# Attention, soft routing and feed-forward in one kernel: another order of loads and steps, and the last weight block in column pieces

## Chip, cores and metric

The kernel runs on one core of one Trainium2 chip. The metric is the device time of the program in microseconds. TensorE (PE in the profile) does matmuls and transposes, VectorE (DVE), ScalarE (ACT) and GpSimd (POOL) work on elements, and SyncE (SP) issues the DMA transfers. PEld is PE's loading of the stationary operand.

## What is computed

Three layers follow one another. The first is windowed attention (4 batches, 8 heads, 576 positions, head size 64, window 64), the second a soft mixture of experts with 32 slots over 8 experts, the third a feed-forward layer with 2,048 hidden units. All 2,304 tokens of width 512 go through all three.

```python
scores = q @ k.T / 8;  keep only 0 <= pos_q - pos_k < 64
attn = exp(scores - max) / (sum + 1e-9);  x = attn @ v           # (2304, 512)

logits = x @ phi                                                 # (2304, 32)
d = softmax over the tokens;  slot_input = d.T @ x               # 8 experts x 4 slots x 512
h = maximum(slot_input[e] @ w1[e], 0);  slot_out[e] = h @ w2[e]  # w1 512x1024, w2 1024x512 for each e
c = softmax over the slots;  x = c @ slot_out                    # (2304, 512)

h = x @ w_in;  g = h * sigmoid(1.702 * h);  out = g @ w_out      # w_in 512x2048, w_out 2048x512
```

The softmax over the tokens needs all of attention, and the slots need that softmax. w_in and w_out come as 64-bit floats and are narrowed in the kernel.

## The kernel before

**Attention** runs in 18 steps (`work`): 16 units of one batch and one pair of heads with eight chunks of 64 rows each, and two steps for the ninth chunks. The steps are pipelined by hand: iteration i emits the scores of step i (`emit_s`, mask L315 and products L330 into bank "s"), the transposes of step i-1 (`emit_t`, PE L350, and its copies to `ab` by ACT L351, head 0 into tile `pa`, head 1 into `pl`), exp of head 0 (`emit_e`, ACT L342, with the running maximum `nm` of DVE L335), the transposes of the normalised rows of step i-2 (`xt_step`, PE L403, ACT L407), the values of step i-1 (`emit_pv`, PE L365), exp of head 1, and the normalisation of step i-1 (`emit_norm`, DVE L374 to L384). Pieces of the routing stand at steps by the tables `mid`, `early`, `late` and `post`: logits (PE L449) at 5, 9, 13 and 17, turns of the weights at 6, 10, 14, slots (PE L499) at 7, 11, 15.

**Order.** Every engine works off its instructions in the order in which the code emits them; nothing is scheduled by a planner. All loads are issued by SP, each behind what it waits for: Q and K of a pair (`load_qk`, L229, 512 KB; L231 for the ninth chunks), V (`load_v`, L243, 258 KB), raw blocks of w_in and w_out (`raw_load`, L154, 512 KB), and w1 and w2 (`load_w`, L149), 16 blocks of 1 MB each. A Q/K or V load waits until its buffer, one of three in turn, has been read. `W_AT` says how many weight blocks are issued at the end of each step; the rest go at fixed places of the tail and with each group of w1. A weight block takes one of 16 slots "w", of which three first hold raw blocks (`raws`), or for w2[0] to w2[6] a seventh of the `arena`, in which attention keeps Q, K, V, x and their transposes.

**Raw blocks** of w_in (four) and w_out (`N_WO`, two) are narrowed during attention: `CONV_AT` names the step at which ACT (L161) begins with each, then POOL, then three passes on DVE.

**The tail** (from `rings.update` behind the steps) ends the routing: values and normalisation of step 17, logits of the ninth chunks (`tail_logits`, PE L686), slots, their sum over the batches (`gather`, `acc`), the transposed slot inputs `siT`, and in between the transposes of the combine weights (`sides`; `c_tile`, PE L419, 32 matmuls for each batch). Then come four groups of w1 (`emit_w1`, PE L763), each behind four blocks, and 16 blocks of w2 (`emit_w2`, PE L804) that add up in one bank. The last w2 block is loaded in two halves of its columns. `so_turn` (PE L860) transposes the slot outputs into `soT`, and `emit_m2` and `emit_m1` (PE L893, L878) multiply them with w_in.

**The feed-forward part** runs 48 steps; each has a product L964, the gelu on ACT (L952), its second half on DVE (L977), and the products with w_out into the output banks (`emit_o`, PE L996). The w_out blocks that were not narrowed during attention are narrowed here (`out_a` on ACT L908, `out_b` on DVE L914 and L171 to L179, `out_w` on ACT L932, `out_c` on DVE L935).

## Time and profile before

| | before |
|---|---|
| runs, us | 370.49, 372.44, 372.84; median 372.44 |
| profiled execution, us | 372.59 |
| its span from the first to the last instruction, us | 370.6 |
| PE busy, us | 355.0 (96%) |
| DVE, ACT, POOL busy, us | 237.8, 195.6, 47.4 |
| mean granted TensorE clock | 1.00 |
| moved by DMA, MB | 70.87 |
| first product into the output (PE L996), us | 145.83 |

The profiled execution's own time is 2.0 us more than its span. Times in views count from the span's start. A busy PE in the first 140 us is the sum of many short matmuls and also of pieces that overlap; whether a wait there costs anything is read from the chain of waits and from the transfers.

### The profile page before, as it was taken

To read this page: it belongs to the slowest core of one execution; us is meant where nothing else is said; L and a number is where in the kernel's file an instruction comes from. 1 tells how busy PE (TensorE), PEld (TensorE's weight loads), DVE (VectorE), ACT (ScalarE), POOL (GpSimd) and SP (SyncE) were. 2 spreads that over 40 slices of the span, in tenths; PEclk is the share of its full clock that TensorE was granted. 3 is DMA by queue.
4 is the path that set the end of the run, shared out by engine and by line. 5 is a ranking of instruction groups with operands and counts; after the bars stand their busy time and mean duration, and the time that the engine had idled before them with its cause. 6 is when DMAs were issued, how large, how long until landed. Compare 5 with 4: busy or idle time off the path is not lost.

```text
span 370.6 us, 7867 instructions
## 1 busy us (share of the span) xinstructions
PE 355.0 (96%) x3091; PEld 271.5 (73%) x3091; DVE 237.8 (64%) x518; ACT 195.6 (53%) x498; POOL 47.4 (13%) x92
## 2 busy tenths in 40 slices
PE   6999999999789998999999999999999999999995
PEld 5887777768543325888778887788887888888884
DVE  3566788877356404949485969697968786262624
ACT  3798878879223205765666644555545453333330
POOL 4545666441100000000000000000000000000000
PEclk9999999999999999999999999999999999999999
DMA  7999999999999995314031314131300000031404
GB/s 268 334 404 408 412 413 409 406 381 375 398 385 370 424 392 218 107 57 135 38 113 58 113 57 130 42 113 59 113 0 2 0 0 2 0 136 37 165 6 170
DMA packets 18804, 70.87 MB, mean 191 GB/s; under 512 B 2000, under 2 KB 3408, under 8 KB 14800
## 3 DMA queue, kind: packets, MB, share of 16 engines
q1 hardware_dynamic: 18768, 70.38, 50.1%
q8 instruction: 24, 0.39, 0.4%
q14 instruction: 12, 0.10, 0.1%
HBM read 65.65 MB, written 4.72 MB: 190 GB/s over the span
## 4 chain that ended last, share of the span: by engine, by line
PE 75%; DMA 9%; ACT 8%; DVE 4%; issue 2%; SPq 0%; POOL 0%; DVEq 0%; ACTq 0%; POOLq 0%
PE s L996 18%; PE t L996 17%; PE v L996 17%; DMA w<-in_w_dram 8%; PE m L964 5%; PE v L365 3%; ACT pa L342 3%; PE s L330 3%; PE m L350 2%; DMA arena<-in_qk_dram 2%; ACT pl L351 2%; ACT pa L351 1%; PE m L499 1%; PE m L449 1%; PE s L763 1%
## 5 line engine op out<-in xcount | busy, mean ns | idle before, releaser
L952 ACT ACTIVATE r<-m 128x384 fp32r<-128x384 f32 (+1 forms) x97 | 47.5, 493 | 85.0 <-PE m L964 84.9
L977 DVE TENSOR_TENSOR r<-g,r 128x384 fp32r<-128x384 f32 x96 | 51.4, 554 | 51.3 <-ACT g L952 43.0
L996 PE MATMUL t<-w,r 128*128 128x512 f32 x288 | 75.8, 395 | 0.0
L996 PE MATMUL s<-w,r 128*128 128x512 f32 x288 | 74.3, 392 | 0.0
L996 PE MATMUL v<-w,r 128*128 128x512 f32 (+1 forms) x291 | 73.4, 387 | 0.0
L996 PEld LDWEIGHTS t<-w,r 128*128 128x128 f32 x288 | 53.8, 188 | 14.7 <-issue 4.0
L996 PEld LDWEIGHTS v<-w,r 128*128 128x128 f32 x291 | 54.3, 188 | 11.4
L996 PEld LDWEIGHTS s<-w,r 128*128 128x128 f32 x288 | 52.6, 188 | 8.5
L952 ACT ACTIVATE g<-m 128x384 f32<-128x384 f32 x96 | 47.9, 501 | 0.0
L342 ACT ACTIVATE pa<-s,nm 128x128 f32<-128x128 f32 x140 | 40.7, 399 | 6.2 <-DVE nm L335 5.7
L964 PE MATMUL m<-cT,w 128*128 128x384 f32 (+2 forms) x113 | 25.7, 319 | 0.0
L335 DVE TENSOR_REDUCE nm<-s 128x4 f32<-128x512 f32 x35 | 22.5, 684 | 4.3 <-PE s L330 3.0
L964 PEld LDWEIGHTS m<-cT,w 128*128 128x128 f32 x113 | 20.8, 188 | 4.7 <-DVE w L901 0.6
L350 PE MATMUL m<-ident,pa 128*128 128x128 f32 x144 | 19.6, 279 | 0.0
L351 ACT COPY pa<-m 128x512 f32<-128x512 f32 x18 | 10.5, 586 | 13.7 <-PE m L350 13.6
L350 PEld LDWEIGHTS m<-ident,pa 128*128 128x128 f32 x144 | 15.5, 141 | 3.0 <-issue 2.4
L330 PE MATMUL s<-arena 64*64 64x128 f32 x352 | 13.7, 271 | 2.2 <-POOL rawt L247 1.6
L763 PE MATMUL s<-w,phis 128*32 128x512 f32 x128 | 14.6, 595 | 0.5 <-DVE phis L744 0.5
L384 DVE TENSOR_TENSOR arena<-v,rs 128x256 f32<-128x256 f32 x36 | 13.6, 420 | 0.6
L330 PEld LDWEIGHTS s<-arena 64*64 64x64 f32 x352 | 11.4, 133 | 3.5 <-POOL rawt L247 2.0
L365 PE MATMUL v<-arena,pa 128*64 128x65 f32 x184 | 13.2, 227 | 0.3 <-issue 0.3
L1016 DVE TENSOR_TENSOR w<-s,w 128x512 f32<-128x512 f32 x18 | 11.6, 684 | 2.8 <-PE s L996 2.8
(206 smaller groups left out, 472.7 us busy)
## 6 DMA issues: line engine op xcount, KB each, us to landing
w<-in_w_dram SPq DMA_DIRECT2D x24, 1024.0 KB, 10.4
w<-in_w_out_dram SPq DMA_DIRECT2D x16, 512.0 KB, 3.4
arena<-in_w_dram SPq DMA_DIRECT2D x7, 1024.0 KB, 8.5
iraw<-in_w_in_dram SPq DMA_DIRECT2D x12, 512.0 KB, 3.3
arena<-in_qk_dram SPq DMA_DIRECT2D x10, 512.0 KB, 8.7
out_dram<-w SPq DMA_DIRECT2D x16, 256.0 KB, 2.1
arena<-in_vt_dram SPq DMA_DIRECT2D x13, 258.5 KB, 7.5
rawt<-in_qk_dram SPq DMA_DIRECT2D x6, 512.0 KB, 9.9
```

What stands on the lines that cost most here:

```text
L330: nc.tensor.matmul(st[h][rows[j], c, :], q, k, start=False, stop=(c == 3), tile_position=(64 * h, 64 * j))
L335: nc.vector.tensor_reduce(out=nm[:, h], in_=st[h], axis=AX.X, op=ALU.max, negate=True)
L342: nc.scalar.activation(out=pb[h][:, c, :], in_=st[h][:, c, :], func=ACTF.Exp, bias=nm[:, h, c:c + 1], scale=1.0)
L350: nc.tensor.transpose(tt[:, c, :], pb[h][:, c, :], ident)
L351: nc.scalar.copy(ab[h], tt)
L365: nc.tensor.matmul(pvt[i][h][64 * j:64 * j + 64, c, :], ab[h][:, c, 64 * j:64 * j + 64], v, start=True, stop=True, tile_position=(0, 64 * j))
L384: nc.vector.tensor_tensor(out=o, in0=pv[h][:, :, 1 - h:65 - h], in1=rs[:, h].unsqueeze(2).to_broadcast([128, 4, 64]), op=ALU.mult)
L763: nc.tensor.matmul(ph[32 * j:32 * j + 32, :], siT[:, kk, :], w1t[4 * r + j][:, kk, :], start=(kk == 0), stop=(kk == KD - 1), tile_position ...
L952: nc.scalar.activation(out=(gh, g)[part][:, a:e], in_=ph[:, a:e], func=ACTF.Gelu_apprx_sigmoid)
L964: nc.tensor.matmul(ph[:, c - a:e - a], mst[:, f * 128:f * 128 + 128], cT(c, e - c), start=True, stop=True)
L977: nc.vector.tensor_tensor(out=gl, in0=g, in1=gh.bitcast(F32), op=ALU.subtract)
L996: nc.tensor.matmul(accs[t][:, h], a[:, c], b[:, h], start=(first and k == 0), stop=(last and k == 2 and h.stop == 512))
```

## The change

- **Values.** `emit_pv` runs over the heads outside and the chunks inside.
- **Start.** The loads are issued in the order qk0, qk1, v0, qk2, v1. The scores of step 2 (with `scale_q(2)` on DVE in place of POOL) stand ahead of the values of step 0, and the three filler matmuls of that place are gone.
- **Raw blocks.** `N_WO` is 1. Two raw blocks are loaded ahead of the steps, two behind step 0 and one behind step 1. `CONV_AT` begins at steps 3, 5, 7, 9 and 11.
- **Weights by step.** `W_AT` gives none at step 10, two at 15, two at 16 and three at 17.
- **Arena.** X0, QK0, XT0, V0, X1, XLT0 and XL0 are each at the start of a seventh; the small tiles fill what is left, some move to `rawt`.
- **Tail.** The values of step 17 stand ahead of the transposes of the combine weights. For three batches `c_wide` spreads the weights with one DVE copy and four full transposes take the place of 32 narrow matmuls. Slots come behind the second tail logits; `acc` is scaled on ACT, and `siT` is copied in two halves by ACT and DVE.
- **Last w2 block.** It is laid out on the host by 128 columns and loaded in pieces of 256, 128 and 128 columns. Blocks 0 to 13 add up in one bank, which ACT copies; blocks 14 and 15 go by pieces into three banks, DVE adds them to the copy, and `so_turn` follows by pieces. The two `warm` matmuls are gone.
- **Feed-forward start.** Block 1 of w_out is narrowed where block 2 was, blocks 2 and 3 in steps 0 to 2.

```diff
-W_AT = {i: 1 for i in range(2, 16)}
-W_AT.update({16: 1, 17: 2})
+PIECES = (slice(0, 2), slice(2, 3), slice(3, 4))
+W_AT = {**{i: 1 for i in range(2, 17)}, 10:0, 15:2, 16: 2, 17: 3}
-CONV_AT = {2 + 2 * n: n for n in range(6)}
+CONV_AT = {i: n for n, i in enumerate((3, 5, 7, 9, 11))}
-N_WO = 2
+N_WO = 1
+X0, QK0, XT0, V0, X1, XLT0, XL0 = [2048 * n for n in range(7)]
...
     load_qk(0)
+    load_qk(1)
     load_v(0)
-    load_qk(1)
+    load_qk(2)
     load_v(1)
...
-        for c in range(4):
-            for h in range(2):
+        for h in range(2):
+            for c in range(4):
                 for j in range(2):
...
+            def c_wide():
+                c = rawt[:, 512 * b:512 * b + 512].rearrange(
+                    "p (t j s) -> p t j s", t=TM, j=4)
+                nc.vector.tensor_copy(c, l.unsqueeze(2).to_broadcast([128, TM, 4, NS]))
+                st["c", 0] = c
...
     for i in range(ns):
-        emit_s(i)
-        if i == 1:
-            for _ in range(3):
-                nc.tensor.matmul(bank("v")[:, 0:128], ident, ident, start=True, stop=True)
+        if i != 2:
+            emit_s(i)
...
+        if i == 1:
+            scale_q(2, nc.vector)
+            emit_s(2)
         if i:
             emit_pv(i - 1)
...
-    load_w(1)
     emit_t(ns - 1)
     xt_step(ns - 2)()
     dexp()
-    sides[0][0]()
-    emit_pv(ns - 1)
...
+    sides[0][3]()
+    emit_pv(ns - 1)
+    emit_norm(ns - 1)
+    load_w(1)
...
     tail_logits(1)
...
-    sides[1][0]()
+    psl = slots()
+    load_w(2)
+    sides[0][0]()
...
+    def next_w2(c, tag):
+        w = slice(128 * c.start, 128 * c.stop)
+        pq = bank(tag)[:, 0:w.stop - w.start]
+        pqs.append(pq)
+        for j in range(4):
             nc.tensor.matmul(
+                pq[32 * j:32 * j + 32], ht_of(14, j), w2t[14][:, j, w], start=True, stop=False,
+                tile_position=(0, 32 * j))
+
+    def last_w2(c):
+        w = slice(128 * c.start, 128 * c.stop)
+        pq = pqs[PIECES.index(c)]
+        for j in range(4):
+            nc.tensor.matmul(
+                pq[32 * j:32 * j + 32], ht_of(15, j), w2t[15][:, c, j], start=False, stop=True,
+                tile_position=(0, 32 * j))
+        nc.vector.tensor_tensor(out=so[:, w], in0=pq, in1=so[:, w], op=ALU.add)
...
-    so_copy()
-    warm(W[0])
-    so_turn(0)
-    so_turn(2)
-    out_a(2)
+    nc.scalar.copy(so, po)
+    for c, tag in zip(PIECES, "mmv"):
+        next_w2(c, tag)
+    for c in PIECES:
+        last_w2(c)
+    so_turn(PIECES[0], "t", nc.scalar.copy)
+    so_turn(PIECES[1], "t", nc.vector.tensor_copy)
+    so_turn(PIECES[2], "s", nc.vector.tensor_copy)
     m0 = emit_m2(0, "s")
+    out_a(1)
```

Three places show how instructions move. A row is a line of the code, the operation, the tiles that it writes and reads, and its shape; "x8" counts equal ones in a row. Line numbers of the kernel after differ a little.

On PE at the start, before: the last scores of step 1 (L330), the filler (L608), the transposes and values of step 0 (L350, L365), and then the scores of step 2 (L315, L330).

```order
L330 MATMUL m<-arena 64x128 x2
L608 MATMUL v<-ident 128x128 x3
L350 MATMUL m<-ident,pa 128x128 x8
L365 MATMUL v<-rawt,pa 64x65 x2
L365 MATMUL v<-rawt,pl 64x65 x2
```

On PE at the same place, after: L327 are scores, L347 transposes, L312 the mask, L362 values.

```order
L327 MATMUL m<-arena 64x128 x2
L347 MATMUL m<-ident,pa 128x128 x8
L312 LDWEIGHTS arena
L312 MATMUL s<-arena 64x512
L312 LDWEIGHTS arena
L312 MATMUL s<-arena 64x512
L312 LDWEIGHTS arena
L312 MATMUL s<-arena 64x512
L312 LDWEIGHTS arena
L312 MATMUL s<-arena 64x512
L327 MATMUL s<-arena 64x128 x16
L362 MATMUL v<-rawt,pa 64x65 x8
L362 MATMUL v<-rawt,pl 64x65 x8
```

The sixteen score pairs of step 2 stand ahead of the values of step 0, which now take all of head 0 (`pa`) and then all of head 1 (`pl`); before, they changed between the heads every two.

On SP from step 13 to the last weight block, before: V loads (L243), ninth chunks (L231) and weight blocks (L149).

```order
L231 DMA rawt<-in_sq_dram 128x768
L243 DMA arena<-in_vt_dram 128x517
L149 DMA w<-in_w_dram 128x2048
L243 DMA rawt<-in_vt_dram 128x517
L149 DMA w<-in_w_dram 128x2048 x2
L149 DMA arena<-in_w_dram 128x2048 x7
L149 DMA w<-in_w_dram 128x2048 x8
L149 DMA w<-in_w_dram 128x4x256 x2
```

On SP at the same place, after: L239, L227 and L145 are the same loads.

```order
L227 DMA rawt<-in_sq_dram 128x768
L239 DMA arena<-in_vt_dram 128x517
L145 DMA w<-in_w_dram 128x2048 x2
L239 DMA rawt<-in_vt_dram 128x517
L145 DMA w<-in_w_dram 128x2048 x2
L145 DMA arena<-in_w_dram 128x2048 x7
L145 DMA w<-in_w_dram 128x2048 x8
L145 DMA w<-in_w_dram 128x1024
L145 DMA w<-in_w_dram 128x512 x2
```

One weight block more stands between the two last V loads, and the last block is three transfers in place of two.

On PE at the last w2 blocks, before: w2 (L804), filler (L755), transposes (L860), m2 (L893).

```order
L804 MATMUL v<-w,rawt 32x512 x32
L804 MATMUL v<-w,rawt 32x256 x8
L755 MATMUL s<-ident 128x128 x2
L860 MATMUL t<-i_82,acc 128x128 x4
L893 MATMUL s<-wi,rawt 128x128 x4
```

On PE at the same place, after: w2 blocks to 13 (L812), block 14 and block 15 by pieces (L871, L879), transposes (L887), m2 (L921).

```order
L812 MATMUL v<-w,rawt 32x512 x28
L871 MATMUL m<-w,rawt 32x256 x4
L871 MATMUL m<-w,rawt 32x128 x4
L871 MATMUL v<-w,rawt 32x128 x4
L879 MATMUL m<-w,rawt 32x256 x4
L879 MATMUL m<-w,rawt 32x128 x4
L879 MATMUL v<-w,rawt 32x128 x4
L887 MATMUL t<-i_82,acc 128x128 x3
L887 MATMUL s<-i_82,acc 128x128
L921 MATMUL s<-wi,rawt 128x128 x4
```

Behind the last piece stand four matmuls of 128 columns, and one of the four transposes has the last piece to wait for.

## Rows read from the trace of the kernel before

**Rows 1.** The page's 40 slices of 9.3 us: granted clock, and what DMA moved.

```profile
PEclk9999999999999999999999999999999999999999
...
GB/s 268 334 404 408 412 413 409 406 381 375 398 385 370 424 392 218 107 57 135 38 113 58 113 57 130 42 113 59 113 0 2 0 0 2 0 136 37 165 6 170
```

**Rows 2.** Chain that ended last, 80 to 146 us: start us, us, what.

```profile
107.24 3.64 PE s L763 x32
...
122.38 17.95 DMA w<-in_w_dram
...
140.37 0.64 PE v L804 x8
...
142.30 0.43 DVE rawt L862
...
142.78 1.16 PE s L893 x8
```

**Rows 3.** Timeline, 139 to 162 us: start us, us, engine, line, op, out<-in; [idle before <-releaser].

```profile
145.83 1.37 PE L996 MATMUL s<-w,r 128*128 128x512 f32 x4
...
149.16 0.42 DVE L914 TENSOR_SCALAR wf<-wf 128x512 f32<-128x512 f32 x1
...
152.09 0.69 DVE L179 SCALAR_TENSOR_TENSOR wf<-w,wf 128x512 uint32<-128x512 uint32 x1
...
160.10 0.49 ACT L952 ACTIVATE r<-m 128x384 fp32r<-128x384 f32 x1 [2.81 <-PE m L964]
...
161.01 0.56 DVE L977 TENSOR_TENSOR r<-g,r 128x384 fp32r<-128x384 f32 x1 [3.12 <-ACT g L952]
```

**Rows 4.** By stretches: busy us of PE, PEld, DVE, ACT, POOL; PEclk, DMA share, GB/s.

```profile
10.00:20.00 10.00, 9.53 (x176) 8.16 (x174) 6.10 (x17) 8.17 (x24) 5.55 (x13) 1.00 0.96 338
20.00:80.00 60.00, 56.87 (x1086) 44.86 (x1083) 46.66 (x130) 50.43 (x156) 34.07 (x55) 1.00 1.02 410
80.00:90.00 10.00, 9.90 (x193) 8.03 (x192) 7.40 (x22) 6.93 (x22) 1.34 (x6) 1.00 0.94 347
...
106.00:118.00 12.00, 11.53 (x102) 4.28 (x105) 7.50 (x17) 3.11 (x6) 0.00 (x0) 1.00 0.96 359
118.00:131.00 13.00, 13.00 (x118) 4.72 (x114) 4.20 (x9) 3.19 (x6) 0.00 (x0) 1.00 1.01 422
```

**Rows 5.** Waits of SP's queue: line, releaser: us in total, times, longest us.

```profile
SPq L243 <- PE v L365: 42.0, 16, 4.3
```

**Rows 6.** Timeline of PE, 0 to 30 us.

```profile
9.41 1.03 PE L608 MATMUL v<-ident 128*128 128x128 f32 x6
...
13.01 0.41 PE L315 MATMUL s<-arena 64*64 64x512 bf16 x4
...
17.07 0.47 PE L315 MATMUL s<-arena 64*64 64x512 bf16 x4
...
19.81 0.34 PE L365 MATMUL v<-arena,pa 128*64 128x65 f32 x4
```

**Rows 7.** Chain that ended last, 12 to 32 us.

```profile
20.22 1.04 PE v L365 x28
...
21.67 0.87 PE s L330 x32
...
24.18 1.16 ACT pa L342 x4
```

**Rows 8.** Timeline, 92 to 108 us.

```profile
94.72 0.85 PE L419 MATMUL s<-ident,lg 128*32 128x128 f32 x20 [1.30 <-issue]
```

**Rows 9.** Timeline of SP (DMA issues), 0 to 150 us.

```profile
81.67 0.33 SPq L243 DMA_DIRECT2D arena<-in_vt_dram  x1
```

**Rows 10.** DMA issues in 81 to 86.5 us: KB each, us to landing.

```profile
arena<-in_vt_dram SPq DMA_DIRECT2D x1, 258.5 KB, 4.2
```

**Rows 11.** Timeline of PE's weight loads, 120 to 141 us.

```profile
137.47 0.16 PEld L804 LDWEIGHTS v<-w,rawt 128*32 128x32 f32 x8 [1.00 <-DMA w<-in_w_dram]
138.88 0.16 PEld L804 LDWEIGHTS v<-w,rawt 128*32 128x32 f32 x8 [1.25 <-DMA w<-in_w_dram]
```

More of the change, by code (lines that the diff above doesn't have):

```diff
@@ L71 @@
 LS0 = NE * 260
+D0, LT0, DT0 = LS0 - 152, LS0 + 288, LS0 + 416
 FP = 4
@@ L147, in load_w @@
                 v = src[i].rearrange("p (a f) -> p a f", a=4)
-                for c in HALVES if plan == [] else (slice(0, 512),):
-                    nc.sync.dma_start(out=t[:, :, c], in_=v[:, :, c])
+                if not plan:
+                    t, v = [x.rearrange("p a f -> p (a f)").rearrange(
+                        "p (c a f) -> p c a f", c=4, a=4) for x in (t, v)]
+                for c in PIECES if not plan else (slice(0, 4),):
+                    nc.sync.dma_start(out=t[:, c], in_=v[:, c])
                 lst.append(t)
@@ L415, in xt_step @@
         return evac
-    def c_tile(p, l):
-        for j in range(4):
-            nc.tensor.matmul(
-                p[32 * j:32 * j + 32], l, ident, start=True, stop=True, tile_position=(0, 32 * j))
     def c_high(a, p):
@@ L460, in lmax @@
                 nc.vector.tensor_tensor(out=al, in0=m, in1=run["m"], op=ALU.subtract)
-                st["al"] = al
+                st["al"] = run["al"] = al
             run["m"] = m
@@ L585, in attention_softmoe_ffn @@
         sides.append(side(0, b * MT, "stv"[b]))
-    load_qk(2)
     nc.sync.dma_start(out=phis, in_=phi.rearrange("p (k s) -> p k s", k=KD))
     raws = [wslot() for _ in range(3)]
+    for n in range(2):
+        early_load(n)
     ns = len(work)
@@ L713, in attention_softmoe_ffn @@
         nc.tensor.transpose(pd[:, t, :], ltt[0:32, t * 128:t * 128 + 128], ident[0:32, 0:32])
+    sr = sp.tile([128, 1], F32, tag="srun", name="srun")
+    nc.vector.tensor_tensor(out=sr, in0=run["s"], in1=al, op=ALU.mult)
+    al3 = sp.tile([128, 1], F32, tag="al3", name="al3")
+    nc.vector.tensor_tensor(out=al3, in0=run["al"], in1=al, op=ALU.mult)
     nc.vector.tensor_copy(dt, pd)
-    pl = bank("m")
+    pm = bank("m")
+    nc.tensor.matmul(pm[:, 0:1], i4m, sr, start=True, stop=True)
+    pl = bank("v")
     for c in range(2):
@@ L721, in attention_softmoe_ffn @@
                 start=True, stop=True, tile_position=(0, 32 * g))
-    load_w(2)
-    sr = sp.tile([128, 1], F32, tag="srun", name="srun")
-    nc.vector.tensor_tensor(out=sr, in0=run["s"], in1=al, op=ALU.mult)
-    pm = bank("m")
-    nc.tensor.matmul(pm[:, 0:1], i4m, sr, start=True, stop=True)
-    nc.vector.tensor_scalar(out=acc, in0=acc, scalar1=al, scalar2=None, op0=ALU.mult)
+    load_w(1)
+    nc.scalar.activation(out=acc, in_=acc, func=ACTF.Copy, scale=al3)
     rsl = sp.tile([128, 1], F32, tag="rsl", name="rsl")
@@ L734, in attention_softmoe_ffn @@
         out=i4s, in0=i4m[:, 0:NS], scalar1=rsl, scalar2=None, op0=ALU.mult)
+    nc.vector.scalar_tensor_tensor(
+        out=acc, in0=psl, scalar=al, in1=acc, op0=ALU.mult, op1=ALU.add)
     siT = phis
+    sides[1][0]()
+    for k in range(2):
+        sides[k][1]()
     sides[2][0]()
@@ L743, in attention_softmoe_ffn @@
                 psi[:, kk, :], acc[:, kk * 128:kk * 128 + 128], i4s, start=True, stop=True)
-    nc.vector.tensor_copy(siT, psi)
-    sides[1][1]()
+        (nc.vector.tensor_copy if k else nc.scalar.copy)(
+            siT[:, 2 * k:2 * k + 2], psi[:, 2 * k:2 * k + 2])
     sides[2][1]()
@@ L782, in attention_softmoe_ffn @@
     turn(1)
-    for f in sides[1][2:] + sides[2][2:] + norm:
+    for f in sides[1][2:3] + sides[2][2:3] + norm:
         f()
@@ L799, in emit_w2, with ht_of @@
     def emit_w2(i):
-        e, hf = divmod(i, 2)
-        for c in HALVES if i == 15 else (slice(0, 512),):
-            for j in range(4):
-                fc = hf * 4 + j
-                nc.tensor.matmul(
-                    po[32 * j:32 * j + 32, c], ht[:, e * 256 + fc * 32:e * 256 + fc * 32 + 32],
-                    w2t[i][:, j, c], start=(i == 0), stop=(i == 15 and c.stop == 512),
-                    tile_position=(0, 32 * j))
+        for j in range(4):
+            nc.tensor.matmul(
+                po[32 * j:32 * j + 32], ht_of(i, j), w2t[i][:, j], start=(i == 0),
+                stop=(i == 13), tile_position=(0, 32 * j))
+    def ht_of(i, j):
+        e, hf = divmod(i, 2)
+        a = e * 256 + (hf * 4 + j) * 32
+        return ht[:, a:a + 32]
     wparts, wraw, wfs = [], [None] * N_WO, {n: wof[:, n, :] for n in range(N_WO)}
@@ L1027, in emit_o @@
                 q()
-    ahead = {10: [lambda: out_w(0)], 11: [lambda: out_c(0), lambda: out_w(1)],
-             12: [lambda: out_c(1)]}
-    wb = bank("s")
-    for i in range(16):
+    ahead = {10: [lambda: out_w(0)], 11: [lambda: out_c(0)]}
+    for i in range(14):
         emit_w2(i)
@@ L1149, in _layout @@
     w2 = moe_w2.reshape(8, 2, 4, 128, 512).transpose(0, 1, 3, 2, 4).reshape(16, 128, 2048)
+    last = w2[15:].reshape(1, 128, 4, 4, 128).transpose(0, 1, 3, 2, 4).reshape(1, 128, 2048)
+    w2 = np.concatenate([w2[:15], last])
     wi = moe2_w_in.reshape(4, 128, 4, 512).transpose(2, 0, 1, 3).reshape(16, 128, 512)
```

107 lines of the change are left out of this document (52 added, 55 removed), and 2 rows, old and new, of the table todo.

## Prediction

> **What bounds the kernel now.** I first read the page in 40 slices of 9.3 us [rows 1]. The granted clock is 9 tenths or more in every slice, its higher level of 2.4 GHz, so no slice is slow for its clock. Transfers run at 370 to 424 GB/s for most of the first 15 slices, some 140 us, and are thin after. So there are two stages: up to 140 us all weights come in over one stream, and after it TensorE works the feed-forward part without pause.
>
> The chain of waits shows the seam [rows 2]: a w1 group of 3.64 us from 107.24, and then nothing but transfers until a landing at 122.38 + 17.95 = 140.32. The last w2 block on PE follows at 140.37, and m2, the product that opens the feed-forward part, at 142.78. The first product into the output runs at 145.83 [rows 3], 5.51 us after the landing. From there to the end PE is the bound and the change touches only its first steps, so what is gained before 145.83 comes off the end.
>
> What sets the landing? Weight bytes as such don't: the table by stretches [rows 4] shows 410 GB/s at 20 to 80 us and 422 at 118 to 131, but 338 at 10 to 20, 347 at 80 to 90 and 359 at 106 to 118. Against 410, 410 and 422 these lose 10 x (1 - 338/410) = 1.76, 10 x (1 - 347/410) = 1.54 and 12 x (1 - 359/422) = 1.79 us, together 5.1. SP, which issues every load in program order, waits 42.0 us in all (16 times) for value matmuls, PE L365, ahead of V loads [rows 5]. A waiting V load holds up every weight behind it. So the landing is set by how early the attention steps release their buffers, and by how early the tail releases the w slots.
>
> **The change part by part.**
>
> *Scores of step 2 ahead of values of step 0.* Scores of step 2 start at 13.01, behind the values of step 0, and those of step 3 at 17.07, a whole step of 4.06 later [rows 6]. Ahead of the values PE ran six records of filler (1.03 us at 9.41, removed) while it waited for copies and V. The scores of step 2 now stand in that place, so they no longer lie between the values of step 0 and the transposes of step 1, and all later steps move up by about their length, which is about the filler's: I take 1.1 us. The load order goes with it: qk0, qk1, v0, qk2, v1. If qk2 lands so late that PE waits for it there, the gain is 0; more than the score matmuls' own length, 0.41 [rows 6] and 0.87 in a later step's chain [rows 7], it can't be.
>
> *Values head by head.* In a plain step the values begin at 19.81 [rows 6] and stop after four matmuls for the copy of head 1; the other 28 take 1.04 from 20.22 to 21.26 [rows 7]. All 32 at this rate are 1.19, so head by head, where head 0's sixteen cover the wait, they can end at 21.00, 0.26 earlier. But in a plain step the next scores also wait for a bank that exp of head 0 frees, a step later at 24.18 + 1.16 = 25.34 [rows 7], just when that step's values end, so there the gain is 0. It counts where routing matmuls (logits, or the turns of weights) stand between values and scores, since there PE is last: steps 5, 6, 9, 10, 13 and 14 before the load that matters below. 6 x 0.26 = 1.6. Bounds: 0, if exp or the running maximum is late there too, and 14 x 0.26 = 3.6.
>
> *One raw block fewer in attention, and weights at other steps.* One 0.52 MB block (1.25 us at 420 GB/s) and its conversion leave the first 130 us. No w block goes at step 10, two at 15, two at 16, three at 17. That takes load off the middle, where the stream was full, and puts two blocks, 5 us of work for the stream, ahead of the second V load that SP waits for in the stretch 80 to 90.
>
> *The tail.* The order of pieces puts the values of step 17 ahead of two blocks of transposes: 20 matmuls of 0.85 us at 94.72 behind a 1.30 us pause [rows 8], and twelve ahead of the pause. So these values move up by a good 2 us, and the slots go behind the tail logits. The wide copy that lets 4 transposes stand for 32 small ones is a DVE pass over 128x512, three times; the nearest row, 0.69 for a DVE pass of that shape with two inputs [rows 3], is the most for it, and it runs beside PE. The w1 groups, from 107.24 before [rows 2], come some 3 us earlier by these transposes alone (0.85, 1.30, and twelve more at the same rate, 0.5), and the arena slots for w2 come free in the order in which they are loaded. I cost this at the gap it closes, the 1.79 of 106 to 118.
>
> *The sum to the landing.* I go by SP's order from the V load at 81.67 [rows 9], which is released by step 14's values. It took 4.2 us to land [rows 10]. Behind it stand one more V load (0.65 at 410 GB/s) and now 20 blocks of 1.049 MB, 2.48 us each at 422. If SP then never leaves the stream empty, the landing is 81.67 - x + 4.2 + 0.65 + 20 x 2.48 = 136.1 - x, where x is what attention gains by step 14: 1.1 + 1.6 = 2.7, of which I take 2.5, since a step that is not the one shown may have another release. Landing at 133.6, so -6.7. The other way of counting, 140.32 less the three gaps of 5.1 less the raw block of 1.25, gives 134.0. PE is no new bound there: it waited for each of the last landings, 1.00 us for the first of them [rows 11], and the w1 start moves with the steps (2.5) and by the tail's 3 us, as much as the landing.
>
> *The last block in pieces of 256, 128 and 128 columns.* After the last landing before: 0.64 of matmuls, copies by ACT, eight transposes, a copy, then m2 (1.16) ending at 143.94, 3.62 after it [rows 2]. Now: four matmuls of a quarter (0.32), an add on DVE and a copy of a quarter each (0.25 each; a copy of two quarters took 0.43 at 142.30), one transpose and the last quarter of m2 (0.3 each, of eight records in 1.16) [rows 2], with six hand-overs of 0.05: 1.7. That is 1.9 less; the third landing costs some of it. The last whole block and the two halves start on PE at 137.47, 138.88 [rows 11] and 140.37 [rows 2]: 1.41 and 1.49 apart, where half a block by rate is 1.24, so a piece costs about 0.2 more than its bytes. With 0.2 for it and 0.2 for the transposes of the first pieces that PE does ahead of the last one, I take -1.5 (bounds 0 and -1.9).
> The Trainium skill says otherwise (SBUF — State Buffer, The DMA setup-cost knee): each transfer pays about 2 us that don't depend on its size. By that rule a third piece would cost 2 us in a row and eat the gain. The two landings above bear on it: 1.4 us apart, they show it hidden behind the transfer before.
>
> *Feed-forward start.* The raw block left out is converted here: on DVE two passes of 0.42 and three of 0.69, 2.91, and on ACT two, which I take as long as the longer DVE pass, 1.38 [rows 3]; 4.3 in all. In the first steps DVE idles 3.12 before 161.01 and ACT 2.81 before 160.10 [rows 3], so most is hidden; the extra cast stands ahead of a gelu on ACT and I charge 0.3. Without cover it is 4.3.
>
> **Sum.** -6.7 - 1.5 + 0.3 = -7.9 on the profiled execution's 372.59 us: 364.7. The median of the runs is 372.44, 0.15 less, which I leave.
>
> **The rivals.**
> - *Attention gets no faster.* What if exp on ACT, not PE, releases each step, and the early scores only move the wait? Then x is about 0.5: 136.1 - 0.5 = 135.6, -4.7 - 1.5 + 0.3, 366.7; if a gap of the size of the one at 106 to 118 stays too (1.79), 368.5. For it: in the plain step ACT's 1.16 does end with PE's values.
> - *The stream is fed throughout.* If the V load finds the stream empty, and lands in 2 us less than its 4.2, and x is 2.7: 131.4, and the end at 362.5. For it: raw blocks go out at once. Against it: loads still need buffers.
> - *Slower: the conversions bind the start of the feed-forward part.* Three w_out blocks instead of two are now converted in steps 0 to 2, in DVE's and ACT's order ahead of the gelus. Each is 4.3 us; were all three on the path, 12.9 instead of 0.3 gives 377.3. It decides against the change once products wait 7.9 us more, and by over 1% from 11.6. Against it: the idle time of both engines above.
> - *Each piece pays in full.* If each of three pieces takes the 1.49 that a half took, however few its bytes, the third adds 1.5 to the forecast: 366.2. Against it: a half already takes little more than its bytes.
> By the 2 us of the Trainium skill's page above it would be an estimated 366.7.
> - *The clock.* Ten filler records are gone. If PE, idle between landings, came to the feed-forward part at the lower level of 1.2 GHz, the stretch from m2 to the first product, 142.78 to 145.83, could take up to 3.05 us more: 367.8. Against it: in every slice the granted clock is full though PE waited as here.
> The Trainium skill has such a rule (TensorE: Matmul & The Clock Gate, Part 1): the clock falls when the engine is little used. No row here shows a fall.
>
> **How the numbers follow.** Forecast (363 to 366.5): 0.50. Attention no faster: 0.26, half of it beyond 368.7. Fed throughout: 0.09. Conversions: 0.07, of it 0.05 slower than now. Pieces in full: 0.04. Clock: 0.04, half of it within 1%, should the lower level last a little longer. About 1% is what a measurement of this kernel can tell from none: faster therefore means under 368.7. Faster: 0.50 + 0.13 + 0.09 + 0.04 + 0.02 = 0.78; within 1%: 0.13 + 0.02 + 0.02 = 0.17; slower 0.05. The predicted time is 364.7. The range goes from 361.5, a little under the fed stream, to 369.0, over the rivals at 366.7 to 368.5; what lies beyond is most of the conversions and little else.
>
> **What would show it.** Scores of step 3 start near 16 instead of 17.07; the V load of 81.67 issues near 79; the stretches 80 to 90 and 106 to 118 run near 410 GB/s; the last landing is near 133.6 and the first product 4.0 behind it; PE shows no wait over 0.5 in the first five steps. I am wrong if the V load still issues at 81 or later, if SP's waits ahead of weight loads come back at other places, or if the first steps of the feed-forward part stretch.

## Result, and the profile after

The changed kernel took 366.89 us (median of 4 runs, 365.33 to 368.03) against 371.73 us of the kernel before beside it (370.49 to 372.84): a ratio of 0.9864, 95% interval 0.9818 to 0.991. Run again beside the experiments it gave 0.9897 (0.9858 to 0.9936). So it is faster by 1.0 to 1.4%, some 4 to 5 us; 7.9 us were forecast. The time lies in the range of 361.5 to 369.0, above the forecast's own range of 363 to 366.5.

| profiled execution | before | forecast | after |
|---|---|---|---|
| time, us | 372.59 | 364.7 | 368.03 |
| span, us | 370.6 | | 366.3 |
| V load behind step 14's values is issued | 81.67 | 79.2 | 80.83 |
| first w1 group starts | 107.24 | | 102.73 |
| last weight landing | 140.32 | 133.6 | 136.7 |
| first product into the output | 145.83 | 137.6 | 141.37 |
| from there to the end | 224.8 | 225.1 | 224.9 |

The page of the kernel after, in the same 40 slices as [rows 1] (now 9.2 us each): granted clock, and what DMA moved.

```profile
PEclk9999999999999999999999999999999999999999
...
GB/s 288 405 413 402 409 389 241 406 340 395 421 415 421 419 407 289 111 64 171 9 107 57 146 27 173 1 116 57 115 2 0 0 2 1 0 153 21 171 3 172
```

The clock is full throughout. The second slice is better than before (405 for 334), the seventh worse (241 for 409). The table by stretches of the kernel after has the columns of [rows 4].

```profile
10.00:20.00 10.00, 9.47 (x193) 7.80 (x195) 6.39 (x19) 8.69 (x28) 3.36 (x8) 1.00 1.02 405
20.00:80.00 60.00, 55.97 (x1076) 43.77 (x1072) 44.72 (x127) 49.65 (x153) 33.14 (x56) 1.00 0.97 375
80.00:90.00 10.00, 9.62 (x210) 8.08 (x206) 7.55 (x25) 7.96 (x26) 0.60 (x4) 1.00 0.97 362
...
106.00:118.00 12.00, 12.00 (x107) 4.29 (x107) 7.41 (x16) 4.12 (x7) 0.00 (x0) 1.00 1.01 416
```

Two of the three gaps are closed as forecast: 10 to 20 us rose from 338 to 405 GB/s, 106 to 118 from 359 to 416. The third hardly changed (347, now 362). And the long stretch fell from 410 to 375: 60 x (1 - 375/410) = 5.1 us, as much as the three gaps of before together. Where it was lost stands in the timeline of SP, the kernel after:

```profile
54.28 0.33 SPq L239 DMA_DIRECT2D rawt<-in_vt_dram  x1
56.32 0.33 SPq L225 DMA_DIRECT2D arena<-in_qk_dram  x1
60.75 0.33 SPq L239 DMA_DIRECT2D arena<-in_vt_dram  x1
61.13 0.42 SPq L145 DMA_DIRECT2D w<-in_w_dram  x1
...
80.83 0.33 SPq L239 DMA_DIRECT2D arena<-in_vt_dram  x1
```

Behind the V load at 54.28 no weight block follows (`W_AT[10]` is 0), so between 56.32 and 60.75 nothing new is issued, and the stretch 56 to 64 us ran at 209 GB/s. The last row is the load at which the forecast's sum began; it was issued 0.84 us earlier than in [rows 9], not 2.5.

The chain that ended last, the kernel after, by the columns of [rows 2]: the w1 group, the two landings, and what follows the last of them.

```profile
102.73 3.57 PE s L774 x32
...
107.20 14.40 DMA w<-in_w_dram
...
121.62 15.08 DMA w<-in_w_dram
...
136.75 0.43 PE v L879 x8
137.18 0.66 PE t L887 x4
...
137.90 0.38 ACT rawt L890
...
138.32 1.16 PE s L921 x8
```

The last landing is at 121.62 + 15.08 = 136.70, 3.6 us earlier. m2 ends at 139.48, 2.78 behind it instead of 3.62, and the first product runs at 141.37, 4.67 behind it instead of 5.51. So the 4.3 us by which the span is shorter are 3.62 + 0.84 - 0.16.

The 3.6 belongs to this pair of traces. In a second trace of the kernel before (b_same, below) the last landing is at 137.0, only 0.3 behind the one here. Over the two traces of the kernel before (140.3, 137.0) and the four whose code is that of the changed kernel up to the last weight block (136.7, 136.7, 133.2, 134.6) the mean landing moved from 138.7 to 135.3.

### The profile page after: what moved, and what is told of

Read it like the earlier page. It is cut to its first block, busy times and chain, and to the rows that moved or that the text cites. A ratio compares the mean times of both kernels' runs of the same rounds, so it can differ in the third digit from the quotient of the medians.

```text
span 366.3 us, 7736 instructions
## 1 busy us (share of the span) xinstructions
PE 353.0 (96%) x3021; PEld 269.8 (74%) x3021; DVE 240.1 (66%) x527; ACT 196.5 (54%) x499; POOL 44.6 (12%) x90
## 4 chain that ended last, share of the span: by engine, by line
PE 76%; DMA 11%; ACT 5%; DVE 5%; issue 2%; POOL 0%; DVEq 0%; SPq 0%; ACTq 0%; POOLq 0%
PE s L1024 18%; PE t L1024 18%; PE v L1024 17%; DMA w<-in_w_dram 8%; PE m L992 5%; PE s L327 4%; PE m L347 3%; ACT pa L339 3%; PE v L362 2%; DMA rawt<-in_sq_dram 2%; PE s L312 2%; DVE nm L332 1%; PE m L400 1%; PE s L774 1%; DMA rawt<-in_qk_dram 1%
## 5 line engine op out<-in xcount | busy, mean ns | idle before, releaser
L347 PE MATMUL m<-ident,pa 128*128 128x128 f32 x144 | 20.6, 282 | 0.3 <-ACT pa L339 0.3
L347 PEld LDWEIGHTS m<-ident,pa 128*128 128x128 f32 x144 | 15.7, 140 | 4.6 <-PE s L327 1.9
L327 PE MATMUL s<-arena 64*64 64x128 f32 x352 | 14.6, 273 | 0.9 <-issue 0.8
L960 ACT CAST w<-wf 128x512 fp32r<-128x512 f32 x15 | 9.3, 623 | 9.3 <-DVE wf L175 9.3
L963 DVE TENSOR_TENSOR w<-wf,w 128x512 fp32r<-128x512 f32 x15 | 10.3, 688 | 5.2 <-ACT w L960 5.1
```

The source lines that it names most:

```text
L327: nc.tensor.matmul(st[h][rows[j], c, :], q, k, start=False, stop=(c == 3), tile_position=(64 * h, 64 * j))
L347: nc.tensor.transpose(tt[:, c, :], pb[h][:, c, :], ident)
```

## Experiments

All but one are the changed kernel with one or two parts undone or altered. V(14) is the V load that step 14's values release, "last V to w1" the time from the issue of the last V load to the first w1 group. Both, and the landing, are those of the one profiled execution. "Low clock" counts the executions whose mean granted clock is 0.995 or less, with the median of the others behind it; the others all have 0.997 or more.

| kernel | median us (runs) | ratio to before (95%) | V(14) | last V to w1 | landing | landing to first product | low clock; median of the others |
|---|---|---|---|---|---|---|---|
| before, first trace | | 1 | 81.7 | 21.5 | 140.3 | 5.5 |  |
| before, second (b_same) | 369.41 (1) | | 81.3 | 20.1 | 137.0 | 5.5 | 0 of 1 |
| changed, first trace | 366.89 (4) | 0.9864 (0.982 to 0.991) | 80.8 | 18.1 | 136.7 | 4.7 | 0 of 4; 366.89 |
| changed, second (a_same) | 367.27 (6) | 0.9897 (0.986 to 0.994) | 81.4 | 18.9 | 136.7 | 4.7 | 0 of 6; 367.27 |
| a_w10 | 368.15 (12) | 0.9926 (0.989 to 0.996) | 80.1 | 19.2 | 134.7 | 4.8 | 8 of 12; 366.28 |
| a_best | 368.00 (12) | 0.9922 (0.989 to 0.995) | 80.3 | 19.2 | 133.9 | 6.2 | 8 of 12; 366.69 |
| a_pv | 365.93 (6) | 0.9881 (0.984 to 0.992) | 78.7 | 17.6 | 134.2 | 4.7 | 1 of 6; 365.93 |
| a_turn | 365.46 (6) | 0.9868 (0.983 to 0.990) | 78.0 | 18.5 | 133.2 | 4.7 | 1 of 6; 365.44 |
| a_turnpv | 366.69 (6) | 0.9893 (0.986 to 0.993) | 79.3 | 18.6 | 136.8 | 4.7 | 0 of 6; 366.69 |
| a_start | 368.45 (12) | 0.9944 (0.992 to 0.997) | 81.2 | 18.2 | 137.9 | 4.7 | 1 of 12; 368.39 |
| a_attold | 366.18 (6) | 0.9891 (0.986 to 0.992) | 80.0 | 19.1 | 134.0 | 5.4 | 0 of 6; 366.18 |
| a_half | 368.16 (12) | 0.9942 (0.992 to 0.997) | 79.0 | 17.8 | 134.6 | 5.5 | 4 of 12; 367.71 |
| a_now | 398.21 (1) | | 77.4 | 17.9 | 165.0 | 6.4 | 1 of 1 |

The table shows first that one trace is one draw. a_turn and a_half do the same as the changed kernel up to the last weight block, and yet V(14) lies between 78.0 and 81.4 in these four traces. So differences of a microsecond or two between two traces prove nothing alone; what follows rests on what repeats in several, or on medians. It shows also that medians are not alike in the clock: a_w10 and a_best ran at a lower mean clock in eight of their twelve executions (0.988 to 0.995), a_half in four, the changed kernel in none of its ten. In a_w10 and a_best every one of the eight took longer than each of the other four (367.49 to 370.09 and 367.63 to 370.35 us, against 364.68 to 367.37 and 365.68 to 367.19). Only one execution of each kernel was traced, none of the eight among them, so where their clock fell, and whether it is the cause of the longer time or follows from a wait, stays open.

**The changed kernel once more (a_same).** No edit.

> The changed kernel once more, as the base for the three beside it. Both theories: 0.982 to 0.991 of the time before, last weight landing at 136.7 and first output product at 141.4, each within 1.5 us, since the four runs so far have spans from 363.5 to 366.3.

0.9897, with landing and first product as in the first trace. As expected; it is the base for the others.

**A block at step 10 (a_w10).**

```diff
-W_AT = {**{i: 1 for i in range(2, 17)}, 10:0, 15:2, 16: 2, 17: 3}
+W_AT = {**{i: 1 for i in range(2, 17)}, 15: 2, 16: 2, 17: 2}
```

> The changed kernel with one weight block at step 10 again, and two instead of three at step 17; steps 15 and 16 keep two. Theory A: in the changed kernel nothing moves from 59.5 to 61.5 us because step 10 issues no block while SP waits for the V buffer; with a block there the 20 to 80 us stretch rises from 375 to about 400 GB/s, the last landing comes 2.0 us earlier (134.7) and the end 1.5 to 2.0 us earlier. Rival B: the idle of the stream only moves, because the same V load still waits; a new pause of 1.5 to 2 us shows up between 80 and 95 us, and the landing stays within 0.5 of 136.7.

Stretches of a_w10, by the columns of [rows 4]:

```profile
20.00:80.00 60.00, 55.58 (x1084) 43.67 (x1076) 45.14 (x126) 49.79 (x154) 33.00 (x57) 1.00 1.01 397
56.00:64.00 8.00, 6.50 (x129) 4.80 (x133) 5.62 (x17) 5.91 (x18) 4.29 (x6) 1.00 0.90 334
80.00:90.00 10.00, 9.48 (x195) 7.82 (x195) 7.97 (x25) 7.54 (x24) 0.60 (x4) 1.00 0.96 343
```

The pause at 60 us shrinks (334 for 209 GB/s) and the long stretch recovers to 397, as theory A said. 80 to 90 us falls back to 343, but in this execution nothing is given back by it: the landing is at 134.7, the first product 4.8 behind it, and it took 366.30 us, 1.7 less than the changed kernel's traced one (368.03). All that is theory A's, though one trace is one draw, and the same code up to the last block landed between 133.2 and 136.7 without the edit. The median is not better: 0.9926 against 0.9864 and 0.9897. It holds the eight executions with the lower clock; the other four have a median of 366.28, against 366.92 of the changed kernel's ten, which four executions can't tell apart. So rival B's stream that gives the gain back is not what the trace shows, and whether the pause costs anything stays open.

**One block a step, and the transposes moved (a_best).**

```diff
-W_AT = {**{i: 1 for i in range(2, 17)}, 10:0, 15:2, 16: 2, 17: 3}
+W_AT = {**{i: 1 for i in range(2, 17)}, 17: 2}
...
-    for c in PIECES:
-        last_w2(c)
-    so_turn(PIECES[0], "t", nc.scalar.copy)
-    so_turn(PIECES[1], "t", nc.vector.tensor_copy)
+    last_w2(PIECES[0])
+    last_w2(PIECES[1])
+    so_turn(PIECES[0], "t", nc.scalar.copy)
+    last_w2(PIECES[2])
+    so_turn(PIECES[1], "t", nc.scalar.copy)
```

> The changed kernel with one weight block at each step from 2 to 16 and two at 17, and the transposes of the first piece ahead of the last piece's matmuls. Theory A: the stream has no pause at 60 us, and TensorE's chain from the first w1 group (33.3 us to m2 at the least) becomes the bound in place of the landing; the end is 0.5 to 1.5 us earlier than the changed kernel, 0.982 to 0.987 of the time before. Rival B: the time that the stream loses only moves, and the end is that of the changed kernel within 0.5.

Chain that ended last, a_best, from the first w1 group on:

```profile
103.31 3.57 PE s L774 x32
...
107.38 3.57 PE s L774 x32
...
111.53 3.57 PE s L774 x32
...
116.13 3.57 PE s L774 x32
...
133.38 0.65 PE m L871 x16
...
137.27 0.89 PE s L921 x8
```

No landing is in the chain any more: TensorE's own work from the first w1 group leads up to m2, 34.0 us (33.3 in the traces of a_w10 and a_attold, the least of all). The landing is at 133.9, but the first product comes only 6.2 us later. So the mechanism of theory A is there: of the 2.8 us by which the landing is earlier than in the changed kernel, 1.3 reach the first product (140.05), and the execution took 366.68 us. The median isn't better (0.9922), again with eight executions at the lower clock. With a block at every step, the w1 groups start at 103.1 to 103.2 in a_w10, a_best and a_attold; without one at step 10, at 100.2 to 104.0 in the seven traces with the new tail and weights in the other steps. That TensorE's chain takes back what the stream gains is thus seen in part in a_best, not in a_w10, where landing and TensorE are ready at the same time, and not shown as a rule.

**The order of the values (a_pv).** In `emit_pv`, the loop over the chunks outside and over the heads inside, as before.

> The changed kernel with the values in the old order, chunks outside and heads inside. Theory A: the order is worth nothing, since exp or the running maximum releases the next scores: V loads and the last landing stay within 0.3 us, the end within 0.5. Rival B, the forecast's term: 0.26 us for each of six steps, so the V load of 80.8 us is issued 1.6 later and the landing comes 1 to 1.6 later.

0.9881 with V(14) at 78.7, among the earliest. Rival B's later load is not there; theory A's 0.3 us isn't met either, since V(14) comes 2.1 earlier, within the spread above. The order brings no gain that can be seen. A plain step, from two rows of SP in the changed kernel:

```profile
24.46 0.33 SPq L239 DMA_DIRECT2D rawt<-in_vt_dram  x1
...
28.58 0.33 SPq L239 DMA_DIRECT2D arena<-in_vt_dram  x1
```

They are 4.12 us apart, and in the kernel before the same two loads were issued at 25.46 and 29.58, 4.12 apart as well. The wait inside the values is gone, but the step is no shorter, as the forecast had it for plain steps. The test is the six steps with routing matmuls (5, 6, 9, 10, 13 and 14), to each of which it gave 0.26. From V load to V load these six together take 33.0 to 34.7 us in the five traces with the old order (the two of before, a_pv, a_turnpv, a_attold) and 33.4 to 36.2 in the eight with the new one and weights in the steps. Step 10 repeats best: 5.29 to 5.35 with the old order, 5.59 or more with the new one; step 11 gives it back, 3.75 to 3.79 against 4.05 or more. So the order moves time from one step to the next. One place where it goes is in the waits of PE, the kernel after (us in total, times, longest):

```profile
PE s L312 <- ACT pa L339: 0.2, 1, 0.2
```

The next scores wait for exp on ACT. This wait, of 0.2 to 0.4 us, is in all nine traces with the new order and in none of the five with the old one: values that end earlier find exp not ready.

**The start (a_start).** Old load order, scores of step 2 behind the values of step 0, filler matmuls back.

> The changed kernel with the old start: loads in the order qk0, v0, qk1, v1, qk2, scores of step 2 behind the values of step 0, and the three filler matmuls. Theory A: the early scores are the one part that moves the steps; the V loads of steps 1 to 4 are issued 1.0 later (near 21.2, 25.4 and 29.5), but the gain is given back by stalls of the middle steps, so the end moves by less than 0.7. Rival B, the forecast's term: all later steps and the last landing come 1.1 later, the end near 368.2.

V loads at 21.0, 25.3 and 29.2, some 0.7 later than in the changed kernel's first trace, and a ratio of 0.9944 against 0.9897 and 0.9864, that is 1.7 to 3.0 us slower (1.2 to 1.6 by the medians). The landing is 1.2 later than in the changed kernel's traces. Rival B holds: on its own, the start is worth about its term. Only 0.7 of it is seen in the early loads, and V(14), 81.2, lies between the changed kernel's two (80.8 and 81.4).

**The whole attention part as before (a_attold).** The edits of a_pv and a_start together, and a weight block at each step from 2 to 16 and two at 17.

> The changed kernel with the attention part as before: old start, old order of the values, one weight block at each step from 2 to 16 and two at 17; tail, arena, last block in pieces and one raw block fewer stay. Theory A: what the change gains comes from the tail (first w1 group 3.7 us sooner after the scores of step 17) and the pieces (0.85), so this one is still 0.985 to 0.993 of the time before, the end at most 1 us behind the changed kernel. Rival B, the forecast's terms: 2.5 us of attention are lost, the end near 369.5.

0.9891, the same as the changed kernel (theory A), though its start is the old one. So the three changes to the attention steps (start, order of the values, weights by step) together bring nothing that can be measured: 366.18 us against 366.89 and 367.27. Together with a_start this leaves one thing unexplained: the old start costs time with the new weight steps and none with the old ones. Its landing is early (134.0) and TensorE late, 5.4 us to the first product, as in a_best. So with this table the landing does not bind, which may be all; that was not tested.

**The last block in halves (a_half).** Two transfers, one bank, ACT's copies, as before.

> The changed kernel with the last w2 block in two halves of its columns, added up in the one bank, as before. Both theories: the first output product again 5.3 to 5.5 us behind the last landing instead of 4.66. By the forecast's term of 1.5 the end is 1.5 later (368.4), by the trace of the changed kernel 0.85 later (367.7). If each transfer cost 2 us of its own, as one rival had it, the landing would come 2 us earlier here (134.7) and the end 1.2 earlier.

0.9942, that is 1.7 to 2.9 us slower by the ratios (0.9 to 1.3 by the medians), and 5.5 us from the landing to the first product. Without its four executions at the lower clock the median is 367.71, 0.8 above the changed kernel's ten. The pieces are worth the 0.84 that the trace shows, or a little more. Timeline of PE at the last three landings, a_half:

```profile
131.69 1.07 PE L810 MATMUL v<-w,rawt 128*32 128x512 f32 x8 [1.05 <-DMA w<-in_w_dram]
133.18 0.64 PE L810 MATMUL v<-w,rawt 128*32 128x256 f32 x8 [0.42 <-DMA w<-in_w_dram]
134.66 0.64 PE L810 MATMUL v<-w,rawt 128*32 128x256 f32 x8 [0.85 <-DMA w<-in_w_dram]
```

The halves are 1.49 and 1.48 apart. The three pieces of the changed kernel landed faster for their size. Issues of the changed kernel in 116.5 to 117, 119 to 119.5 and 121.5 to 122 us (KB, us to landing):

```profile
w<-in_w_dram SPq DMA_DIRECT2D x1, 512.0 KB, 18.7
w<-in_w_dram SPq DMA_DIRECT2D x1, 256.0 KB, 16.9
w<-in_w_dram SPq DMA_DIRECT2D x1, 256.0 KB, 15.1
```

Issued at 116.68, 119.12 and 121.62, they landed at 135.4, 136.0 and 136.7: the two quarters 0.6 to 0.7 apart, their bytes at 422 GB/s (0.62) and little more. The halves of before are cut across each partition's rows; the new layout on the host makes every piece one run for each partition. I take that for the cause of the 0.2 us for each half, but it was not tried by itself.

**The transposes of the first piece ahead (a_turn).** The second edit of a_best alone.

> The changed kernel with the transposes of the first piece ahead of the last piece's matmuls on TensorE. Theory A: in the changed kernel these transposes and ScalarE's copy stand behind the last landing, and m2 starts 1.6 us after it; with them ahead, m2 starts 1.0 to 1.2 us after the landing and the first output product 4.0 to 4.2 instead of 4.66; the end is 0.5 earlier. Rival B: the path behind m2 (ScalarE's cast, the second group, the gelus) decides anyway, and the first output product stays 4.5 to 4.7 behind the landing.

Timeline of PE, a_turn:

```profile
133.15 0.71 PE L887 MATMUL t<-i,acc 128*128 128x128 f32 x4 [0.16 <-DVE acc L882]
133.79 0.43 PE L879 MATMUL v<-w,rawt 128*32 128x128 f32 x8
...
134.95 1.06 PE L921 MATMUL s<-wi,rawt 128*128 128x128 f32 x8
```

From the last piece's matmuls to m2 it takes 1.16 us instead of 138.32 - 136.75 = 1.57, so the transposes were in the way. But the moved transposes wait for DVE's add and start only at 133.15, just as the last piece lands (133.2), so TensorE comes to that piece 0.6 us late, and the first product is again 4.7 behind the landing. That is rival B's figure, by another way. a_turnpv repeats it with a landing of 136.8: TensorE comes to the piece at 137.41. The ratio is 0.9868, no different from the changed kernel's.

**Both (a_turnpv).** The edits of a_turn and a_pv.

> The changed kernel with two edits: values in the old order, and the transposes of the first piece ahead of the last piece's matmuls. Theory A: they add up, as the first is worth nothing or a little against the new order and the second 0.4: the end near 365.5, 0.983 to 0.987 of the time before. Rival B: the order of the values is worth its term and the end is near 367.

0.9893: they don't add up to anything that can be measured.

**No weights in the attention steps (a_now).** `W_AT = {16: 2, 17: 2}`.

> The changed kernel with no weight block ahead of step 16 (two at 16, two at 17): the weights then come 13 blocks late, so the end is some 25 to 33 us later; only the attention steps are of interest. Theory A: the Q, K and V loads of steps 10 to 16 no longer queue behind weight blocks, and the pauses of the middle steps go: the V load issued at 80.8 in the changed kernel comes at 77 or earlier. Rival B: the steps are set by TensorE, ScalarE and VectorE; that load is issued between 79 and 82 as before.

V(14) at 77.4, and w1 at 99.0: short of the 77 that theory A named, but earlier than in any kernel with weights. Q, K and V do queue behind weight blocks: between 40 and 60 us a Q/K load of 512 KB takes a median of 3.5 us from issue to landing here and 7.0 in the changed kernel. Over the five traces with the changed kernel's attention part (80.8, 81.4, 78.0, 79.0, and 79.1 in a_oldtail) the mean of V(14) is 79.7, 2.3 later than here. That this is what the blocks cost is likely but not shown: it is one trace, 0.6 ahead of the earliest of the five.

The trace shows the clock as well. Where the w2 blocks come one by one, TensorE works some 1.07 us on each and then waits up to 1.44. By stretches, and two of these blocks:

```profile
120.00:140.00 20.00, 12.80 (x85) 3.35 (x83) 3.50 (x8) 2.07 (x4) 0.00 (x0) 1.00 1.01 418
140.00:165.00 25.00, 17.18 (x100) 3.20 (x104) 0.00 (x0) 0.58 (x1) 0.00 (x0) 0.64 1.01 417
```

```profile
138.11 1.06 PE L812 MATMUL v<-arena,rawt 128*32 128x512 f32 x8 [1.43 <-DMA arena<-in_w_dram]
140.61 1.94 PE L812 MATMUL v<-arena,rawt 128*32 128x512 f32 x8 [1.44 <-DMA arena<-in_w_dram]
```

The granted clock fell from 1.00 to 0.50 just behind 140 us and rose again at 147; a block took 1.94 us in place of 1.06.

**The kernel before once more (b_same).** No edit.

> The kernel before once more, for a second trace of its attention steps. Theory A: its first trace (372.59 us) was on the slow side of its runs: the V load of 81.67 is issued 0.5 to 2 us earlier here and the last landing lies 0.5 to 2.5 earlier, at the same 29.4 us behind the end of the first w1 group. Rival B: the attention steps repeat within 0.3 us, and the difference between runs comes from elsewhere.

V(14) is at 81.3, 0.4 earlier, between the two theories. The last landing is at 137.0, 3.3 earlier, more than theory A had, and 27.9 behind the end of the first w1 group instead of 29.4. So most of the difference arose behind the attention steps. Timeline of PE, b_same:

```profile
92.69 1.08 PE L419 MATMUL s<-ident,lg 128*32 128x128 f32 x32
...
105.43 2.78 PE L763 MATMUL s<-w,phis 128*32 128x512 f32 x24 [0.48 <-DVE phis L744]
```

The 32 transposes of the first batch run in one piece here, without the pause of 1.30 us in the midst of them [rows 8] that the forecast counted as a price of the old order. It comes and goes: a_oldtail, with the same 32 transposes at this place, has one of 1.06 (PE):

```profile
92.11 0.63 PE L416 MATMUL s<-ident,lg 128*32 128x128 f32 x13 [1.06 <-issue]
```

The stream's loss behind the w1 group is smaller too: 385 GB/s at 106 to 118 us, where the first trace has 359 [rows 4].

**The old tail (a_oldtail).** The order from the transposes of step 17 to `siT` as before, the rest as changed.

> The changed kernel with the order of the tail as before (c_tile with its narrow transposes ahead of the values of step 17, slots ahead of the second tail logits, siT in one copy); attention, arena, weight steps and the pieces stay as changed. Theory A: the tail is the larger part of what the change brings: the first w1 group is again 21 to 21.5 us behind the last V load's issue instead of 18 to 19, the stream pauses again behind it, and the end is 2.5 to 3.5 us later than the changed kernel, near 370 or 0.995 to 1.0 of the time before. Rival B: the stream, fed from 84 us on, hides the tail; w1 starts 3 us later but the landing moves by less than 1 us, the end by less than 1.

This one can't be used for the tail. Its first load behind the steps, w2[3], goes into the seventh that now holds V0; put ahead of the values of step 17, it takes the place of the V rows that they read, so they work on weights, and wait for them. Median 387.42 us, 1.0438 (1.039 to 1.0487). What it does show, in a timeline and by stretches:

```profile
104.78 0.34 PE L362 MATMUL v<-arena,pa 128*64 128x65 f32 x1 [12.04 <-DMA arena<-in_w_dram]
...
109.61 2.08 PE L698 MATMUL s<-arena 128*128 128x128 f32 x8 [2.23 <-DMA arena<-in_w_dram]
```

```profile
93.00:105.00 12.00, 0.22 (x3) 0.26 (x5) 0.00 (x0) 0.00 (x0) 0.00 (x0) 0.59 1.01 423
105.00:110.00 5.00, 2.77 (x36) 2.25 (x36) 1.92 (x9) 0.59 (x1) 0.00 (x0) 0.50 0.51 211
```

TensorE stood for 12 us, its granted clock fell to 0.50, the lower level of 1.2 GHz, and the eight matmuls of the tail logits took 2.08 us instead of the 1.16 that they take in the other traces. How much of the gain the new tail brings is therefore only read from traces: from the last V load to w1 it takes 17.6 to 19.2 us in the eleven traces with the new tail that the table has, and 20.1 and 21.5 in the two with the old one, so about 2.4 us less.

## Why the prediction held, and where it missed

Its direction and its range held, and of its mechanism the end: the last landing set the start of the feed-forward part, it came earlier, and what was gained there came off the end. Its largest new term, what attention gains, did not hold, and the gain was little over half of the one forecast. Two of its own signs of being wrong appeared: the V load is issued at 80.83 and 81.41 in the two traces of the changed kernel, on either side of the 81 that it named, and SP's wait came back at another place, 56 to 61 us. By its own steps:

- **x, what attention gains by step 14** (2.5 taken), is the step that failed. The changed kernel's two traces have 0.84 and 0.26. The order of the values (1.6 of it) is worth nothing: a_pv, a_turnpv and a_attold, with the old order, lie at 0.988 to 0.989, and the six steps that were to gain 0.26 each are no shorter. The forecast had seen that in a plain step exp frees the bank at the same time, and assumed that TensorE was last in the others; it is not, the scores wait for exp there (a_pv). This is the first rival, for the values. Its 366.7 and 368.5 enclose the profiled execution's 368.03; that the forecast set half of its chance beyond 368.7 does not follow from these prices, which are both under it. The other part, the start (1.1), is 1.0 at the loads of 20 to 29 us and over 1 us in the time of a_start, but nothing in a_attold.
- **The sum to the landing** was right as a sum. From the issue at 80.83, with a measured 4.9 to the landing, 0.65 and 20 x 2.48 give 136.0; it was 136.7. So of the 3.1 us by which the landing missed 133.6, 1.7 is x, 0.7 the longer way of the V load, and 0.7 is in neither.
- **The other way of counting, by gaps**, was wrong in form. It took three gaps as closed and none as opened. The changed kernel closes two and opens one of the same size. The gap at 10 to 20 us is closed with the old start too (406 GB/s in a_start), so it isn't the early scores that close it.
- **"PE is no new bound there"** is true of the changed kernel's first trace, where TensorE waits 1.44 us for the block before the last, but only just: in a_best, with the landing 2.8 us earlier, it is the bound. From w1 at 102.7 and the least of 33.3 us, m2 can't start before 136.0, 2.3 ahead of where it does, so a landing 3.1 earlier would not have been worth 3.1 in that execution.
- **The tail** (3 us) had nearly the right size for its part (2.4 by the traces), but 1.30 of it is a pause that the second trace doesn't have (b_same). That execution took 372.59 us, where 17 runs of the same kernel beside the experiments have a median of 371.04, so the forecast set its shorter stream against a late landing.
- **The last block** (-1.5): the trace has -0.84, and a_half loses about that. The pieces did land by their bytes, better than the 0.2 us allowed for each. What was missed is the order on TensorE: all pieces' matmuls stand ahead of all transposes, so the first piece's transposes and ACT's copy lie behind the last landing (137.18 and 137.90 in the chain), and m2 waits for them as a whole. Moving them ahead gains nothing, since DVE's add comes too late for it (a_turn, a_turnpv).
  The Trainium skill (SBUF — State Buffer, The DMA setup-cost knee) gives about 2 us for each transfer; here the pieces followed each other at 0.6 to 0.7 us for 256 KB, so the measurement decides, and in a full queue this cost is not seen.
- **Feed-forward start** (+0.3): 224.93 against 224.77 us, so hidden but for 0.16. The slower rival, conversions that bind, fell.
- **The clock** stayed full in the changed kernel, without the ten filler records: 0.998 or more in each of its ten executions, with waits of 1.4 us at most behind the w1 groups in the traced one. The rival's mechanism exists all the same: the clock fell to 0.50 in a_oldtail, with 12 us of waiting, and in a_now, with waits of no more than 1.44 us, but one behind every w2 block. And eight of twelve executions of a_w10 and of a_best had a mean clock of 0.995 or less.
  The Trainium skill (TensorE: Matmul & The Clock Gate, Part 1) says that the clock is set by how busy TensorE has been; the traces of a_oldtail and a_now agree.

What stays open: what the 4 to 5 us consist of beyond the 0.84 of the pieces. a_attold puts them outside the start, the order of the values and the weights by step, but the tail could not be taken back alone, and the raw block left out and the arena were not tried by themselves. Also why the old start costs over 1 us with the new table of weight steps and nothing with the old one, why the clock falls in so many executions of a_w10 and a_best, and what makes the middle steps differ by up to 3 us between executions of the same code. Pauses of TensorE without a releaser in the profile are part of that: 1.3 us ahead of values in a_same, 2.3 ahead of scores in a_best.

No version tried is clearly faster than the changed kernel; a_turn, at 0.9868, is equal to it.

## What to carry to other kernels

Where one stream brings both the weights of a later stage and the inputs of the present one, a pause in it is not simply a loss: weights put into it queue ahead of the inputs behind them, and TensorE's own chain may take back a part of what the landing gains, as in a_best. Before counting a gap as a gain, work out the second chain, here from the first w1 group to m2 (33.3 us at the least), and see how far behind it lies. And take a second trace of the kernel before, if it can be had: a pause of 1.3 us that stood in the sum was not in the next execution. A median belongs beside the granted clock of its executions: the traced ones of a_w10 and a_best are better than the changed kernel's, and their medians, with eight executions of twelve at a lower clock, are not.

## What the runs showed of the hardware

Transfers of 256 KB at the end of a full queue landed 0.6 to 0.7 us apart; halves of a block cut across the rows of each partition were 1.48 to 1.49 apart, a piece of the same size in whole runs landed 1.3 behind the block before it (134.1 and 135.4 in the changed kernel). TensorE's granted clock fell to 0.50 in a wait of 12 us (a_oldtail), and also in a row of waits of up to 1.44 us, each behind some 1.07 us of matmuls (a_now); single waits of up to 1.44 us in the changed kernel left it at 1.00.
